# Seven half-size products for eight in the last batch's output stage, and one ring of buffers

## The chip, the cores and the metric

The kernel runs on one core of a Trainium2 chip. The metric is the device time of one execution in microseconds: the median of several runs. A profile is one such execution, taken by the hardware profiler; its times are counted from the first instruction.

Engines: PE multiplies matrices and accumulates in PSUM (PEld is its loading of weights, which overlaps the multiplications); DVE works on vectors; ACT does activations and copies; POOL issues most loads here; SP issues the stores and the transposing transfers.

## The reference, cut to what matters

An attention over channels is followed by a gated feed-forward layer. B = 4, N = 5824, C = 256, F = 1024; the output has B * N = 23296 rows of 256.

```python
qn = q / (np.linalg.norm(q, axis=1, keepdims=True) + 1e-06)
kn = k / (np.linalg.norm(k, axis=1, keepdims=True) + 1e-06)
s = kn.transpose(0, 2, 1) @ qn / tau
a = softmax(s, -1)                 # a [C, C] for each batch
x = (v @ a).reshape(B * N, C)
h = ((x @ w1) * (x @ w2)) @ w3     # [B * N, F]
out = (h @ w_out).astype(np.float32)
```

The kernel folds what has no rows in it. The softmax of a batch goes into w1 and w2 (the tile Wf, two matrices of 256 x 1024), and w3 @ w_out is one matrix W of 1024 x 256 (the tile W_sb). What is left for each row is a = v Wf1, b = v Wf2, ab = a * b, out = ab W.

## The kernel before, in words

**Tiles and chunks.** A batch's rows stand in 45 groups of 128 and a rest of 64. A chunk c takes four groups, 512 rows; a batch has eleven such chunks (c = 0 to 10) and a small one (c = 11: the 45th group and the rest). NCH is 12, FT = 8 is the number of blocks of 128 among the 1024 features.

**A slot.** The main loop runs over batches b, chunks c and blocks j = 0 to 7. I call one turn of it a slot. In a slot `emit_ab(b, c, j)` issues four matmuls of 512 columns: a and b for the 128 features of block j, each as a sum over two halves of C. ACT copies a from PSUM to SBUF as bf16 (`as`, L482). DVE multiplies it with b in PSUM and writes ab in bf16 (`abs`, L497): 128 features by 512 rows. The PSUM tag "ab" has four buffers, so a and b of a slot take the place of those two slots earlier; `as` has four buffers.

**The output stage.** `emit_out(b, c, j, ab)` multiplies ab with W: for each of the four groups of rows, ab's 128 x 128 block is loaded as weights and W's 256 columns of block j are streamed (L521). Over the eight j the sums stand in two PSUM tiles of 128 x 2 x 256. After j = 7, ACT copies one (L542) and DVE the other (L543) into `osb`, and SP stores the chunk (L544), 512 KB.

**The order around it.** The order on each engine is the order in which the Python program issues, and tiles' hazards become semaphore waits. Finished ab tiles wait in the list `pend`; a slot pops one when more than LAG = 2 are in it, so the output matmuls of a block stand two slots behind its multiplication. In batch 0, W isn't ready until late, ab tiles pile up, and then two are popped in a slot. In the last two chunks the lag rises to LAG_END = 5, and five entries are left for the end. Other work (loads, the scores and softmax of the next batch, W's computation) is in `agenda`, a list of due times against `clock`, a running sum of planned PE time; `run_due` issues what is due. Loads on POOL stand behind gates (L464, L468): a copy of one element that waits for the newest ab or for a transposed piece.

**Buffers.** q, k and v come in pieces of 1024 rows (4 KB a partition), with 5, 6 and 3 buffers. ab tiles have 34 buffers of 1 KB (tag "ab_sb"); those of the first two chunks take a q buffer for four of them. The transposed w3 takes four k buffers. A buffer is handed out again when the program has issued the last reader of its tile.

Of the kernel before, what the change touches and what calls it, by code (L numbers as in the profile page):

```python
# [12 lines left out]
F32 = DT.float32  # L13
BF16 = DT.bfloat16

P = 128
PIECE = 8
LAG = 2
LAG_END = 5
IN_BUFS = {"q": 5, "k": 6, "v": 3}  # L20
MM_COL = 1.0 / 2400.0
MM_FIX = 0.0025

# [2 lines left out]
def kernel(  # L26
# [12 lines left out]
    nc = tc.nc  # L39

    B, N, C = q.shape
    T, D = out.shape
# [8 lines left out]
    FT = F // P  # L51
    NT = N // P
# [5 lines left out]
    NCH = NT // 4 + 1  # L58
# [6 lines left out]
    in_pool = ctx.enter_context(tc.tile_pool(name="in_pool", bufs=1))  # L65
    vT_pool = ctx.enter_context(tc.tile_pool(name="vT_pool", bufs=2))
    wf_pool = ctx.enter_context(tc.tile_pool(name="wf_pool", bufs=2))
    work = ctx.enter_context(tc.tile_pool(name="work", bufs=2))
    psum = ctx.enter_context(tc.tile_pool(name="psum", bufs=1, space=bass.MemoryType.PSUM))
# [17 lines left out]
    W_sb = consts.tile([P, FT, D], BF16)  # L87
# [12 lines left out]
    pieces = {}  # L100

    def new_piece(nm, n, pi):
        t = in_pool.tile([P, PIECE, C], BF16, tag=nm, name=f"{nm}_{n}_{pi}", bufs=IN_BUFS[nm])
        pieces[nm, n, pi] = t
        if pi == NP_ - 1:
            if nm != "v":
                nc.vector.memset(t[LEFT:, LAST, :], 0.0)
            nc.gpsimd.dma_start(out=t[:LEFT, LAST, :], in_=qk_main[nm, n][1])
# [6 lines left out]
    def load_piece(nm, n, pi, cuts=()):  # L115

        new_piece(nm, n, pi)
        ends = [0, *cuts, LAST if pi == NP_ - 1 else PIECE]
        for lo, hi in zip(ends, ends[1:]):
            load_part(nm, n, pi, lo, hi)  # L120
# [19 lines left out]
    def transpose_half_on_pe(n, pi, h, on_act):  # L140
        if pi == 0 and h == 0:
            new_vT(n)
        t = pieces["v", n, pi]
        i0 = 4 * h
        pe_transpose(
            vTs[n][0][:, pi * PIECE + i0 : pi * PIECE + i0 + 4, :, :].rearrange("p i c t -> p (i c) t"),
            [t[:, i0 + i, ct * P : (ct + 1) * P] for i in range(4) for ct in range(CT)],
            "out", on_act,
        )
# [279 lines left out]
    clock = [0.0]  # L429
# [11 lines left out]
    def at(t, cost, fn):  # L441
        seq[0] += 1
        agenda.append((t, seq[0], cost, fn))
# [3 lines left out]
    pend = []  # L447

    def chunk_cols(c):
        return 4 * P if c < NCH - 1 else P + LEFT  # L450

    def rhs_of(b, c, ct):
        vT, vTt = vTs[b]
        if c < NCH - 1:
            return vT[:, 4 * c : 4 * c + 4, ct, :]
        return vTt[:, ct, :]

    last_ab = [None]
    held = [None]

    def gate():

# [3 lines left out]
    def hold(src):  # L466

        nc.gpsimd.tensor_copy(gate_t, src)  # L468

    def emit_ab(b, c, j):  # L470
        n = chunk_cols(c)
        tiles = []
        for w in range(2):
            t = psum.tile([P, 512], F32, tag="ab", name=f"{'ab'[w]}_{b}_{c}_{j}", bufs=4)
            for ct in range(CT):
                nc.tensor.matmul(  # L476
                    t[:, :n], lhsT=Wf[b][:, ct, w, j * P : (j + 1) * P], rhs=rhs_of(b, c, ct),
                    start=(ct == 0), stop=(ct == CT - 1),
                )
            tiles.append(t)  # L480
        a_sb = work.tile([P, 512], BF16, tag="a_sb", name=f"as_{b}_{c}_{j}", bufs=4)
        nc.scalar.copy(a_sb[:, :n], tiles[0][:, :n])  # L482
        if c == NCH - 1:
            if b % 2 == 0 and j == 0:
                lefts[b // 2] = work.tile([P, FT, 2, P + LEFT], BF16, tag="left", name=f"left_{b}", bufs=1)
            both = lefts[b // 2][:, j, b % 2, :]
            nc.vector.tensor_mul(both, a_sb[:, :n], tiles[1][:, :n])  # L487
            ab = both[:, :P] if b % 2 == 0 else both[:, LEFT:]
        else:
            if b == 0 and c < 2:  # L490

                if j % 4 == 0:
                    held[0] = in_pool.tile([P, 4, 512], BF16, tag="q", name=f"abq_{c}_{j}", bufs=IN_BUFS["q"])
                ab = held[0][:, j % 4, :]
            else:
                ab = work.tile([P, 512], BF16, tag="ab_sb", name=f"abs_{b}_{c}_{j}", bufs=8 * NDEF + 2)
            nc.vector.tensor_mul(ab, a_sb, tiles[1])  # L497
        pend.append((b, c, j, ab))
        last_ab[0] = ab
        clock[0] += 4 * (n * MM_COL + MM_FIX)  # L500

    def emit_out(b, c, j, ab, only=None):
# [42 lines left out]
            if only is None:  # L545
                del out_tiles[b, c]

    NDEF = 4

    def load_qk(n, pi):  # L550
        load_piece("q", n, pi)
        load_piece("k", n, pi)
# [5 lines left out]
    for nm in "kq":  # L558
        new_piece(nm, 0, 0)
        raw[nm] = work.tile([P, half, C], F32, tag="o_sb", name=f"raw_{nm}", bufs=3)  # L560
        first = nc.sync if nm == "k" else nc.scalar
# [8 lines left out]
    def transpose_w3():  # L570

        for h in range(FT // 2):
            m = in_pool.tile([P, 2, FT, P], BF16, tag="k", name=f"w3T_{h}", bufs=IN_BUFS["k"])
            nc.sync.dma_start_transpose(m, w3_bf[:, 2 * h : 2 * h + 2, :])
            w3T.append(m)

# [67 lines left out]
    w_ready = [False]  # L644
# [21 lines left out]
    def make_agenda(b):  # L666
        agenda.clear()
        clock[0] = 0.0
        n = b + 1
        if b == 0:  # L670
            at(0.5, 0.87, soft0[5])
            for i in range(4):
                at((1.7, 2.6, 3.5, 3.9)[i], 0.43, soft0[7 + i])
            at(0.0, 0.0, load_library)
            at(4.6, 0.5, lambda: transpose_half_on_pe(0, 0, 1, False))
            at(7.0, 0.5, lambda: transpose_half_on_pe(0, 1, 0, True))
            at(8.0, 0.5, lambda: transpose_half_on_pe(0, 1, 1, False))
            at(15.0, 0.0, transpose_w3)
            at(15.0, 0.0, lambda: transpose_piece(0, 2))
            for jt in range(FT):  # L680
                at(27.5 + 1.2 * jt, 0.87, lambda jt=jt: w_unit(jt))
            moves = [("qk", 1, 0, 29.0), ("v", 0, 3, 30.0), ("v", 0, 4, 30.5), ("qk", 1, 1, 44.0), ("qk", 1, 2, 45.0)]
            moves += [("qk", 1, 3, 53.0), ("qk", 1, 4, 55.0), ("v", 0, 5, 61.0), ("qk", 1, 5, 73.0)]
            moves += [("v", 1, 0, 88.0), ("v", 1, 1, 98.0), ("v", 1, 2, 120.0), ("qk", 2, 0, 130.0)]
            t0, t1 = 54.0, 113.0
        else:
            moves = [("v", b, 3, 1.0), ("qk", n, 1, 10.0), ("qk", n, 2, 17.0), ("v", b, 4, 26.0), ("qk", n, 3, 38.0)]
            moves += [("v", b, 5, 46.0), ("qk", n, 4, 58.0), ("qk", n, 5, 66.0)]
            moves += [("v", n, 0, 76.0), ("v", n, 1, 86.0), ("v", n, 2, 96.0), ("qk", n + 1, 0, 108.0)]
            moves = [m for m in moves if m[1] < B]  # L690
            t0, t1 = 16.0, 98.0

        before = (0, 2) if b == 0 else None
        for nm, m, pi, t in moves:
            if before is not None and not (nm == "v" and before == (m, pi - 1) == (0, 3)):
                at(t, 0.0, lambda w=before: hold(vTs[w[0]][1][:1, 0, :1] if w[1] == NP_ - 1 else vTs[w[0]][0][:1, w[1] * PIECE, 0, :1]))
            at(t, 0.0, gate)
            if nm == "qk":
                at(t, 0.0, lambda m=m, pi=pi: load_qk(m, pi))
                before = None  # L700
            else:
                at(t, 0.0, lambda m=m, pi=pi: load_piece("v", m, pi))
                at(t + 4.0, 0.0, lambda m=m, pi=pi: transpose_piece(m, pi))
                before = (m, pi)
        if n == B:
            agenda.sort()
            return
        units = score_units(n)
        for i, (cst, fn) in enumerate(units):
            at(t0 + (t1 - t0) * i / len(units), cst, fn)  # L710
        soft = soft_units(n)
        for cst, t, fn in soft:
            at(t1 + 1.0 + t, cst, fn)
        agenda.sort()

    for b in range(B):
        make_agenda(b)
        for c in range(NCH):
            for j in range(FT):
                run_due()  # L720
                emit_ab(b, c, j)
                npop = 0
                lag = LAG
                if b == B - 1 and c >= NCH - 2:
                    lag = LAG_END if c == NCH - 1 else LAG + (LAG_END - LAG) * (j + 1) // FT
                while w_ready[0] and len(pend) > lag and npop < 2:
                    emit_out(*pend.pop(0))
                    npop += 1
                    run_due()
        run_due(1e9)  # L730

    n = len(pend)
    for i, only in [(i, 1) for i in range(n - 1)] + [(i, 0) for i in range(n - 2)] + [(n - 1, 1), (n - 2, 0), (n - 1, 0)]:
        emit_out(*pend[i], only=only)


# [33 lines left out]
```

## Time and profile before

| what | value |
|---|---|
| time, median of 6 runs | 569.57 us (569.38 to 569.7) |
| the profiled execution | 569.68 us, span 567.9 us |
| PE / PEld busy | 556.7 / 355.4 us |
| DVE / ACT / POOL busy | 375.3 / 339.1 / 78.5 us |
| output matmuls (L521) of 256 columns | 1344 + 64 + 48, mean 273 ns |
| a and b matmuls of 512 columns (L476) | 704 + 704, mean 379 ns |
| ab multiplication (L497) | 687 ns |
| copy of a (L482, 512 columns) | 585 ns |
| granted clock of TensorE | 1.000 |

How to read it: a matmul's duration runs from its start to the end of its last result; matmuls that follow each other start closer than that, and the busy time of a group counts the time that they cover together. In rows of the profile the arrow points from what is read to what is written, the shapes are partitions x elements, and "idle before" names what the engine waited for.

### The profile page before, as it was taken

The numbers are of one execution on the slowest core, as the hardware profiler recorded it, in microseconds if no ns is written. First come the engines' busy times: TensorE is split into PE (matmuls) and PEld (weight loads), VectorE is DVE, ScalarE is ACT, GpSimd is POOL, SyncE is SP. The second block draws the span as 40 slices with busy tenths as digits, with TensorE's granted clock in tenths as the row PEclk, the third lists the DMA queues.
The fourth block names the chain that finished last, engine by engine and source line by source line (L and its number), as shares of the span: only waits on it lengthen the run. The fifth ranks groups of instructions, "written<-read, shape, count | busy, mean of one in ns | idle before, by whom it ended". The sixth has DMA issues, their size and how long they took to land.

```text
span 567.9 us, 10088 instructions
## 1 busy us (share of the span) xinstructions
PE 556.7 (98%) x3748; PEld 355.4 (63%) x3755; DVE 375.3 (66%) x581; ACT 339.1 (60%) x627; POOL 78.5 (14%) x163
## 2 busy tenths in 40 slices
PE   8799999999999999999999999999999999999997
PEld 5664576776656666666656666666665666566655
DVE  1047645888966578888766667787876665565564
ACT  1047536777766577777575567777765554454453
POOL 4260013120211010121210101030120000000000
PEclk9999999999999999999999999999999999999999
DMA  9999989978455696595661495765741325221011
GB/s 213 211 178 208 169 173 233 228 165 196 114 146 121 140 194 147 91 191 124 146 149 75 96 220 117 156 120 122 184 113 39 85 74 149 63 66 72 38 69 61
DMA packets 75105, 77.45 MB, mean 136 GB/s; under 512 B 54193, under 2 KB 58801, under 8 KB 75057
## 3 DMA queue, kind: packets, MB, share of 16 engines
q0 software_dynamic: 15760, 38.93, 39.4%
q1 hardware_dynamic: 59008, 37.23, 21.5%
q10 hardware_dynamic: 288, 0.66, 0.4%
q8 instruction: 29, 0.48, 0.4%
q14 instruction: 20, 0.16, 0.1%
HBM read 78.91 MB, written 23.86 MB: 181 GB/s over the span
## 4 chain that ended last, share of the span: by engine, by line
PE 93%; DMA 5%; ACT 1%; POOL 0%; issue 0%; DVE 0%; ACTq 0%; POOLq 0%
PE o L521 28%; PE a L476 28%; PE b L476 28%; PE G L192 5%; DMA k<-in_k_dram 5%; PE fold L363 2%; PE w L649 1%; ACT kr L283 0%; PE quarter L389 0%; POOL k L111 0%; POOL q L111 0%; PE sqk L225 0%; PE tr_I-594_595 L134 0%; PE row L271 0%; ACT e L322 0%
## 5 line engine op out<-in xcount | busy, mean ns | idle before, releaser
L497 DVE TENSOR_TENSOR abs<-as,b 128x512 bf16<-128x512 bf16 x336 | 230.4, 687 | 144.0 <-ACT as L482 131.5
L482 ACT CAST as<-a 128x512 bf16<-128x512 f32 (+1 forms) x384 | 216.3, 563 | 170.1 <-DVE abs L497 84.6
L476 PEld LDWEIGHTS <-Wf 128*128 128x128 bf16 x1536 | 149.1, 98 | 102.2 <-ACT Wf L398 0.7
L476 PE MATMUL a<-vT,Wf 128*128 128x512 bf16 x704 | 209.4, 379 | 0.5 <-ACT Wf L398 0.4
L476 PE MATMUL b<-vT,Wf 128*128 128x512 bf16 x704 | 209.4, 379 | 0.0
L521 PE MATMUL o<-W_sb,abs 128*128 128x256 bf16 x1344 | 201.5, 273 | 0.0
L521 PEld LDWEIGHTS <-abs 128*128 128x128 bf16 x1344 | 131.4, 98 | 79.7 <-issue 0.2
L201 DVE TENSOR_TENSOR acc<-acc,sq 128x1024 f32<-128x1024 f32 x66 | 80.4, 1219 | 0.6 <-ACT sq L189 0.6
L192 PE MATMUL G<-k,q 128*128 128x256 bf16 x276 | 49.7, 273 | 0.0
L189 ACT ACTIVATE sq<-q 128x512 f32<-128x512 bf16 x66 | 41.8, 633 | 0.0
L189 ACT ACTIVATE sq<-k 128x512 f32<-128x512 bf16 x66 | 41.5, 629 | 0.0
L464 POOL COPY gate_t<-abs 1x1 bf16<-1x1 bf16 x39 | 10.5, 270 | 169.4 <-DVE abs L497 167.0
L543 DVE COPY osb<-o 128x512 f32<-128x512 f32 x44 | 30.1, 685 | 0.9 <-PE o L521 0.9
L192 PEld LDWEIGHTS <-q 128*128 128x128 bf16 x276 | 27.0, 98 | 3.1
L542 ACT COPY osb<-o 128x512 f32<-128x512 f32 x44 | 25.8, 586 | 4.0 <-PE o L521 2.1
L468 POOL COPY gate_t<-vT 1x1 bf16<-1x1 bf16 x16 | 3.3, 208 | 162.2 <-DMA vT<-v 162.2
L111 POOL DMA_DIRECT2D q<-in_q_dram x28 | 15.2, 542 | 12.4 <-DMA k<-in_k_dram 5.4
L370 ACT ACTIVATE Wf<-fold,rs 128x512 bf16<-128x512 f32 x15 | 10.3, 687 | 10.9 <-PE fold L363 7.9
L283 ACT ACTIVATE kr<-row 128x256 f32<-128x256 f32 x1 | 0.4, 384 | 26.1 <-PE row L271 26.1
L487 DVE TENSOR_TENSOR left<-as,b 128x192 bf16<-128x192 bf16 x32 | 11.3, 354 | 5.1 <-ACT as L482 2.7
L363 PE MATMUL fold<-w,e 128*128 128x512 bf16 x52 | 14.2, 379 | 0.0
L497 DVE TENSOR_TENSOR abq<-as,b 128x512 bf16<-128x512 bf16 x16 | 10.8, 686 | 5.0 <-ACT as L482 4.5
(98 smaller groups left out, 241.5 us busy)
## 6 DMA issues: line engine op xcount, KB each, us to landing
out_dram<-osb SPq DMA_DIRECT2D x44, 512.0 KB, 3.3
k<-in_k_dram POOLq DMA_DIRECT2D x19, 512.0 KB, 8.5
v<-in_v_dram POOLq DMA_DIRECT2D x19, 512.0 KB, 5.3
q<-in_q_dram POOLq DMA_DIRECT2D x18, 512.0 KB, 6.0
w_wout<-in_moe_w_dram POOLq DMA_DIRECT2D x1, 2048.0 KB, 23.3
k<-in_k_dram POOLq DMA_DIRECT2D x4, 320.0 KB, 7.9
v<-in_v_dram POOLq DMA_DIRECT2D x4, 320.0 KB, 5.0
q<-in_q_dram POOLq DMA_DIRECT2D x3, 320.0 KB, 4.2
```

The source lines that it names most:

```text
L111: nc.gpsimd.dma_start(out=pieces[nm, n, pi][:, lo:hi, :], in_=qk_main[nm, n][0][:, pi * PIECE + lo : pi * PIECE + hi, :])
L189: nc.scalar.activation(out=dst[:, :, part, :], in_=src[:, o : o + 2, :], func=AF.Square)
L192: nc.tensor.matmul(G[:, ct, :], lhsT=qt[:, i, ct * P : (ct + 1) * P], rhs=kt[:, i, :], start=(pr == 0 and part == 0 and ct == 0), stop=(pr ...
L201: nc.vector.tensor_add(accs[n], accs[n], sqs[0])
L363: nc.tensor.matmul(m, lhsT=st["e"][:, c2, c1 * P : (c1 + 1) * P], rhs=w12[:, c2, w, lo:hi], start=(c2 == 0), stop=(c2 == CT - 1),)
L476: nc.tensor.matmul(t[:, :n], lhsT=Wf[b][:, ct, w, j * P : (j + 1) * P], rhs=rhs_of(b, c, ct), start=(ct == 0), stop=(ct == CT - 1),)
L482: nc.scalar.copy(a_sb[:, :n], tiles[0][:, :n])
L487: nc.vector.tensor_mul(both, a_sb[:, :n], tiles[1][:, :n])
L497: nc.vector.tensor_mul(ab, a_sb, tiles[1])
L521: nc.tensor.matmul(tl[h][:, o, :], lhsT=lhsT, rhs=W_sb[:, j, :], start=(j == 0 and o == 0), stop=(j == FT - 1 and (small or o == 1)), skip ...
L542: nc.scalar.copy(o[:, 0:2, :], tl[0])
L543: nc.vector.tensor_copy(o[:, 2:4, :], tl[1])
```

## The change

In chunks 0 to 9 of the last batch the product ab W is formed by a scheme of seven products of half the size for eight (Winograd's form of Strassen's method). ab W is seen as a 2 x 2 block matrix product: A is 512 rows by 1024 features, halved to A11, A12 (256 rows; features 0 to 511, 512 to 1023), A21, A22 (the other 256 rows), and W is halved to B11, B12, B21, B22 (512 features by 128 columns). Each product is four blocks of features times two groups of rows: eight matmuls of 128 columns, with weights of their own, in place of thirty-two of 256 columns for a chunk in all.

- **Sums of ab**: S1 = A21 + A22, S2 = S1 - A11, S3 = A11 - A21, S4 = A12 - S2, four DVE operations on 128 x 1024 bf16. S1 is issued in slot 7 of the chunk itself, S2, S3 and S4 with the products p1, p5 and p7, which stand two, two and three slots ahead of the reader (p6, p7, p3); p5 reads S1.
- **Sums of W** (`combine_weights`): five DVE subtractions and two ACT copies, in four steps that batch 1's agenda has at 3.0, 5.6, 8.2 and 10.8.
- **Products**: in the order p1, p5, p6, p7, p2, p4, p3, one in each of slots 0 to 6 of the next chunk, after that slot's a and b; slot 7 has none. They accumulate in three PSUM tiles: A gets p1, then p6, p7 and p4 on top of each other, C gets p5 and then p3 on top, B gets p2.
- **Quarters of the output**: `keep` copies A (ACT) into a quarter of `osb` after p1, p6, p7 and p4; `join` adds a PSUM tile to a quarter (DVE): B to (0,0) after p2, C to (1,1) in p4's slot ahead of p4, C to (0,1) after p3. Then the chunk is stored as before.
- **The list**: an entry of `pend` now carries the slot from which it may be popped and a size; a slot has room for two; a product has size 2.
- **Buffers**: q, k and v pieces, the transposed w3, ab (now in halves of four blocks, 4 KB) and the sums share one tag of 22 buffers of 4 KB.

The diff, cut:

```diff
-IN_BUFS = {"q": 5, "k": 6, "v": 3}
+BIG_BUFS = 22
...
-        t = in_pool.tile([P, PIECE, C], BF16, tag=nm, name=f"{nm}_{n}_{pi}", bufs=IN_BUFS[nm])
+        t = in_pool.tile([P, PIECE, C], BF16, tag="big", name=f"{nm}_{n}_{pi}", bufs=BIG_BUFS)
...
+    def seven(b, c):
+        return b == B - 1 and c < NCH - 2
+
+    def combine_weights(step):
...
+        if step == 0:
+            nc.vector.tensor_sub(f[:, 0], b12, b11)
+        elif step == 1:
+            nc.scalar.copy(T[:, 0], f[:, 0])
+            nc.vector.tensor_sub(f[:, 1], b22, f[:, 0])
+        elif step == 2:
+            nc.scalar.copy(T[:, 1], f[:, 1])
+            nc.vector.tensor_sub(T[:, 2], b22, b12)
+        else:
+            nc.vector.tensor_sub(T[:, 3], b21, f[:, 1])
+
+    def seven_products(b, c, k1, k2):
...
+        a11, a21 = k1[:, :, : 2 * P], k1[:, :, 2 * P :]
+        a12, a22 = k2[:, :, : 2 * P], k2[:, :, 2 * P :]
...
+        def product(nm, a, w, first=False):
+            if first:
+                st[nm] = psum.tile([P, 2, P], F32, tag="out", name=f"prod{nm}_{b}_{c}", bufs=3)
+            for j in range(4):
+                for i in range(2):
+                    nc.tensor.matmul(
+                        st[nm][:, i, :], lhsT=a[:, j, i * P : (i + 1) * P], rhs=w[j],
+                        start=(first and j == 0 and i == 0), stop=(j == 3), skip_group_check=True,
+                    )
...
+        def keep(r, d):
+            nc.scalar.copy(quarter(r, d), st["A"])
+
+        def join(nm, r, d):
+            nc.vector.tensor_add(quarter(r, d), st[nm], quarter(r, d))
+
+        def sum1():
+            nc.vector.tensor_add(s1, a21, a22)
+
+        def p1():
+            st["o"] = work.tile([P, 4, D], F32, tag="o_sb", name=f"osb_{b}_{c}", bufs=3)
+            nc.vector.tensor_sub(s2, s1, a11)
+            product("A", a11, w1, True)
+            keep(0, 0)
+
+        def p5():
+            nc.vector.tensor_sub(s3, a11, a21)
+            product("C", s1, t1, True)
+
+        def p6():
+            product("A", s2, t2)
+            keep(0, 1)
+
+        def p7():
+            nc.vector.tensor_sub(s4, a12, s2)
+            product("A", s3, t3)
+            keep(1, 1)
+
+        def p2():
+            product("B", a12, w21, True)
+            join("B", 0, 0)
+
+        def p4():
+            join("C", 1, 1)
+            product("A", a22, t4)
+            keep(1, 0)
+
+        def p3():
+            product("C", s4, w22)
+            join("C", 0, 1)
+            rows = out[b * N : b * N + NT * P, :].rearrange("(p i) c -> p i c", i=NT)
+            nc.sync.dma_start(out=rows[:, 4 * c : 4 * c + 4, :], in_=st["o"])
+
+        return [sum1, p1, p5, p6, p7, p2, p4, p3]
...
-            if b == 0 and c < 2:
-
-                if j % 4 == 0:
-                    held[0] = in_pool.tile([P, 4, 512], BF16, tag="q", name=f"abq_{c}_{j}", bufs=IN_BUFS["q"])
-                ab = held[0][:, j % 4, :]
-            else:
-                ab = work.tile([P, 512], BF16, tag="ab_sb", name=f"abs_{b}_{c}_{j}", bufs=8 * NDEF + 2)
+            if j % 4 == 0:
+                halves[j // 4] = in_pool.tile([P, 4, 512], BF16, tag="big", name=f"abh_{b}_{c}_{j}", bufs=BIG_BUFS)
+            ab = halves[j // 4][:, j % 4, :]
             nc.vector.tensor_mul(ab, a_sb, tiles[1])
-        pend.append((b, c, j, ab))
...
+        slot[0] += 1
+        if not seven(b, c):
+            pend.append((slot[0] + LAG, 1, lambda only=None: emit_out(b, c, j, ab, only)))
+        elif j == FT - 1:
+            fns = seven_products(b, c, *halves)
+            fns[0]()
+            pend.extend((slot[0] + 1, 2, fn) for fn in fns[1:])
...
+        if b == 1:
+            for i in range(4):
+                at(3.0 + 2.6 * i, 0.0, lambda i=i: combine_weights(i))
...
-                lag = LAG
+                lag = 0
...
-                while w_ready[0] and len(pend) > lag and npop < 2:
-                    emit_out(*pend.pop(0))
-                    npop += 1
+                room = 2
+                while w_ready[0] and len(pend) > lag and pend[0][0] <= slot[0] and pend[0][1] <= room:
+                    _, size, fn = pend.pop(0)
+                    fn()
+                    room -= size
                     run_due()
```

More of the change, by code (lines that the diff above doesn't have):

```diff
@@ L458 @@
     last_ab = [None]
-    held = [None]
+    halves = [None, None]
+    slot = [0]
+    comb = {}
+    def seven(b, c):
+        return b == B - 1 and c < NCH - 2
+    def combine_weights(step):
+        b11, b12 = W_sb[:, 0:4, :P], W_sb[:, 0:4, P:]
+        b21, b22 = W_sb[:, 4:8, :P], W_sb[:, 4:8, P:]
+        if step == 0:
+            comb["T"] = in_pool.tile([P, 4, 4, P], BF16, tag="big", name="comb_T", bufs=BIG_BUFS)
+            for nm in ("S12", "S34"):
+                comb[nm] = in_pool.tile([P, 2, 4, 2 * P], BF16, tag="big", name=f"comb_{nm}", bufs=BIG_BUFS)
+            comb["f"] = in_pool.tile([P, 2, 4, P], F32, tag="big", name="comb_f", bufs=BIG_BUFS)
+        T, f = comb["T"], comb["f"]
+        if step == 0:
+            nc.vector.tensor_sub(f[:, 0], b12, b11)
[7 more added lines that the diff above has]
+            nc.vector.tensor_sub(T[:, 3], b21, f[:, 1])
@@ new lines, in seven_products, with quarter @@
+    def seven_products(b, c, k1, k2):
+        T = comb["T"]
+        a11, a21 = k1[:, :, : 2 * P], k1[:, :, 2 * P :]
+        a12, a22 = k2[:, :, : 2 * P], k2[:, :, 2 * P :]
+        s1, s2 = comb["S12"][:, 0], comb["S12"][:, 1]
+        s3, s4 = comb["S34"][:, 0], comb["S34"][:, 1]
+        w1 = [W_sb[:, j, :P] for j in range(4)]
+        w21 = [W_sb[:, 4 + j, :P] for j in range(4)]
+        w22 = [W_sb[:, 4 + j, P:] for j in range(4)]
+        t1, t2, t3, t4 = ([T[:, i, j, :] for j in range(4)] for i in range(4))
+        st = {}
+        def product(nm, a, w, first=False):
[7 more added lines that the diff above has]
+                    )
+            clock[0] += 8 * (P * MM_COL + MM_FIX)
+        def quarter(r, d):
+            return st["o"][:, 2 * r : 2 * r + 2, d * P : (d + 1) * P]
+        def keep(r, d):
[32 more added lines that the diff above has]
+        return [sum1, p1, p5, p6, p7, p2, p4, p3]
@@ L546, in emit_out @@
                 del out_tiles[b, c]
-    NDEF = 4
     def load_qk(n, pi):
@@ L572, in transpose_w3 @@
         for h in range(FT // 2):
-            m = in_pool.tile([P, 2, FT, P], BF16, tag="k", name=f"w3T_{h}", bufs=IN_BUFS["k"])
+            m = in_pool.tile([P, 2, FT, P], BF16, tag="big", name=f"w3T_{h}", bufs=BIG_BUFS)
             nc.sync.dma_start_transpose(m, w3_bf[:, 2 * h : 2 * h + 2, :])
@@ L721 @@
                 emit_ab(b, c, j)
-                npop = 0
-                lag = LAG
+                lag = 0
                 if b == B - 1 and c >= NCH - 2:
                     lag = LAG_END if c == NCH - 1 else LAG + (LAG_END - LAG) * (j + 1) // FT
-                while w_ready[0] and len(pend) > lag and npop < 2:
-                    emit_out(*pend.pop(0))
-                    npop += 1
+                room = 2
[3 more added lines that the diff above has]
+                    room -= size
                     run_due()
@@ L733 @@
     for i, only in [(i, 1) for i in range(n - 1)] + [(i, 0) for i in range(n - 2)] + [(n - 1, 1), (n - 2, 0), (n - 1, 0)]:
-        emit_out(*pend[i], only=only)
+        pend[i][2](only=only)
 _INS = ['q', 'k', 'v', 'tau', 'moe_w1', 'moe_w2', 'moe_w3', 'moe_w_out']
```

## The prediction, made before the changed kernel had run

> **What bounds the kernel now.** I read the page first: the busy shares and the chain of waits.
>
> ```profile
> PE 556.7 (98%) x3748; PEld 355.4 (63%) x3755; DVE 375.3 (66%) x581; ACT 339.1 (60%) x627; POOL 78.5 (14%) x163
> PE 93%; DMA 5%; ACT 1%; POOL 0%; issue 0%; DVE 0%; ACTq 0%; POOLq 0%
> ```
>
> PE is busy for 98% of the span and carries 93% of the chain. Next, the windows, to see whether this holds in the last batch, where the products change, and in the early stretch in which PE makes a and b without output products:
>
> ```profile
> 38.00:60.00 22.00, 21.95 (x124) 10.95 (x124) 16.15 (x25) 15.63 (x26) 0.40 (x1) 1.00 1.06 192
> 465.00:490.00 25.00, 25.00 (x155) 14.96 (x153) 15.19 (x23) 12.89 (x22) 0.89 (x3) 1.00 0.33 85
> 490.00:515.00 25.00, 25.00 (x155) 15.04 (x154) 14.31 (x22) 12.59 (x22) 1.26 (x3) 1.00 0.33 93
> ```
>
> Columns: stretch, length, busy PE, PEld, DVE, ACT, POOL, granted clock, DMA share, GB/s. PE has no hole in the last batch and its clock is full, so a microsecond taken from its stream there is a microsecond of the kernel, until another engine is late. To see how late the others run I took the timeline of one slot (one call of emit_ab and one of emit_out):
>
> ```profile
> 480.28 0.59 PE L476 MATMUL a<-vT,Wf 128*128 128x512 bf16 x2
> 480.71 0.59 PE L476 MATMUL b<-vT,Wf 128*128 128x512 bf16 x2
> 480.91 0.59 ACT L482 CAST as<-a 128x512 bf16<-128x512 f32 x1 [0.71 <-DVE abs L497]
> 481.14 0.60 PE L521 MATMUL o<-W_sb,abs 128*128 128x256 bf16 x4
> 481.53 0.69 DVE L497 TENSOR_TENSOR abs<-as,b 128x512 bf16<-128x512 bf16 x1 [0.61 <-ACT as L482]
> 481.58 0.59 PE L476 MATMUL a<-vT,Wf 128*128 128x512 bf16 x2
> ```
>
> Columns: start, length, what. A slot lasts 481.58 - 480.28 = 1.30 us: 0.86 for a and b (four matmuls started 0.216 apart) and 0.44 for four output matmuls 0.109 apart. On a slot clock that starts with a, as runs 0.63 to 1.22 and the multiplication 1.25 to 1.94, 0.64 into the next slot. DVE is then idle for 0.61 us.
>
> **PE's part.** A chunk loses 8 x 4 = 32 matmuls of 256 columns, 32 x 0.109 = 3.49 us, and gets 7 x 8 = 56 of 128 columns, each with weights of its own. The kernel has that shape at its start, in the squares and the transposes:
>
> ```profile
> 26.65 1.06 PE L225 MATMUL sqk<-k 128*128 128x128 bf16 x16
> 43.63 0.61 PE L134 MATMUL tr_I-594_595<-ident_b,v 128*128 128x128 bf16 x8
> ```
>
> One such matmul takes 0.219 us, so 16 of them start (1.06 - 0.219)/15 = 0.056 us apart and 8 of them (0.61 - 0.219)/7 = 0.056, all with different weights, between 512-column matmuls too (the transposes stand between a's and b's). 56 x 0.056 = 3.12 us. Saved: 0.37 us a chunk, 3.7 us in ten. The lower bound of the spacing is this row; the upper one is a weight load that overlaps nothing, 0.098 us by its row, 5.49 us a chunk and 20 us in all. I take 0.056, because the row has the very shape. Break-even is 3.49/56 = 0.062 us.
>
> The Trainium skill speaks against it: "TensorE: Matmul & The Clock Gate", section "Back-to-back issue gap", gives about 81 ns per matmul for a sustained stream of weight loads and 128-column matmuls. By that a chunk's products would take 4.54 us, 1.05 more than now, and the kernel 580 us. The rows of this trace say 56 ns, though in runs of 16 at most.
>
> **DVE's part.** A chunk loses one 684 ns copy and gets four sums of 1024 bf16 numbers and three joins (256 f32 from PSUM plus SBUF). For a join there is a row of the same form, for a sum there is none; the nearest are these:
>
> ```profile
> L317 DVE TENSOR_TENSOR s<-G,kr 128x256 f32<-128x256 f32 x8 | 3.2, 416 | 0.2 <-ACT kr L283 0.2
> L138 DVE COPY vT<-tr_I-496_497 128x1024 bf16<-128x1024 bf16 x1 | 0.7, 693 | 0.0
> L201 DVE TENSOR_TENSOR acc<-acc,sq 128x1024 f32<-128x1024 f32 x66 | 80.4, 1219 | 0.6 <-ACT sq L189 0.6
> ```
>
> So a sum takes between 0.69 (1024 bf16, but a copy) and 1.22 us (1024, two operands, but f32). I take 0.69: the type is the sum's. "VectorE: DVE Perf Modes", section "The perf-mode tier table", of the Trainium skill lists a two-operand bf16 operation from SBUF at twice the f32 rate (1224 ns for 2048); as an estimate that is 0.69 us here.
>
> Busy DVE per chunk: 8 x 0.687 + 4 x 0.69 + 3 x 0.416 = 9.5 us of about 10.1, after 6.2 of 10.4. That is tight, but independent operations start before the one in front ends (a copy follows a multiplication 0.61 us after its start, at 498.43 and 499.04), which brings the sum to 8.3. The order within the chunk decides, so I walk it. Slots 0 to 6 now last 0.86 + 0.45 = 1.31 us, slot 7, without a product, 0.86: a chunk is 7 x 1.31 + 0.86 = 10.03 us. Clock from the start of slot 7:
> - sum1 needs the multiplication just before it, so it starts 0.03 after 1.94 (dependent DVE pairs here start 34 ns after the first ends): 1.97 to 2.66. p5 reads it at 0.86 + 1.31 + 0.86 = 3.03. Spare 0.37.
> - The next multiplication starts at 2.58, 0.5 late; s2 runs 3.19 to 3.88, p6 reads it at 4.34. Spare 0.46.
> - The next is at 3.80; s3 runs 4.41 to 5.10, p7 reads it at 5.65. Spare 0.55.
> - b's buffers are reused two slots on: a multiplication may end 1.09 late (0.66 across slot 7) before PE waits for it; it is 0.5 late.
>
> The joins: in slot 5 the join of C (quarter 1,1) stands behind that slot's multiplication: it starts at 1.25 + 0.61 = 1.86, ends at 2.27, with some 0.04 to the waiter (the step from a's end to as) 2.31. p3 writes C and would start at 1.31 + 0.86 = 2.17. **PE waits 0.14 us** in every chunk. Behind p3 stand the next slot's a and b, so everything after it moves by that: 1.4 us in ten chunks. Below, it could be nothing, if DVE gets to the join earlier; above, 0.26, if it doesn't overlap the multiplication and starts 0.03 after it. The other two joins wait for products that ended 0.4 us before DVE is free, and their readers are slots away.
>
> **ACT's part.** Four keeps of 372 ns (L538's form) for one copy of 586: 0.9 us more a chunk, 6.2 of 10.1. The tightest is p6's: the product ends at 1.31 + 0.16 = 1.47, keep runs 1.51 to 1.88, p7 writes that PSUM tile at 2.17 (spare 0.29) and as of the next slot is due at 1.94. No cost; a keep of 0.586 us would still fit.
>
> **What else moves.** combine_weights: five subtractions (at most 0.69 each) and two ACT copies (about 0.63) in batch 1, one step in 2.6 us; each takes at most DVE's 0.61 of idle time in its slot, and a multiplication has 1.09 of slack. Nothing; 3.1 us if all fell on PE. The ring: I followed the written order and counted the tiles alive. Of 22 buffers at most 17 are in use in batch 0; later 9, and the four of the combined weights. Buffers are handed out in the order in which they came free, so a new tile waits for readers long done. POOL gets no new instruction, its gates stand as before; SP still issues one output transfer a chunk, after the join in slot 6. Before, piece q(0,5) waited for a buffer and now doesn't, but the loads there wait for landings with the DMA at its limit: nothing. Chunk 0 has six slots of 0.86 without output work; the window 38 to 60 shows PE full in such slots. The list of deferred work is again five entries long when the last product starts, so the tail stays.
>
> **The sum.** The profiled execution took 569.68 us (567.9 of span, 1.8 around it), the median is 569.57, so the sum applies to both. 569.57 - 3.7 + 1.4 = **567.3 us**, 0.4% less. With the wait between nothing and 0.26 a chunk: 565.9 to 568.5.
>
> **Rivals.**
> - *Slow sums* (slower): a sum takes the f32 row's 1.22 us. Then s1 ends at 3.19 and p5 waits 0.20; s2 ends at 4.94 against 4.54, 0.44 with the step to PE; s3 at 6.69 against 6.29, 0.44. With p3's 0.14 a chunk is 11.25 us, 0.85 over now: 578 us. It decides from the point at which s3 is late: s3 ends at 3.03 + 3 x (a sum), which meets p7 at 0.86 us, and the whole gain is gone at 0.94. For it: no row with two bf16 operands. Against it: the 693 ns row.
> - *No wait at p3*: 565.9 us. For it: only an overlap larger than the rows show.
> - *New waits eat the gain*: two more waits of p3's size a chunk, from handovers between engines that the walk leaves 0.3 to 0.5 of spare: 567.3 + 2 x 1.4 = 570.1 us, and 568.7 with one. For it: DVE at 94% by durations.
> - *Paced by weight loads*: from 0.062 us on the products cost more than now; halfway to the 0.098 row, at 0.077, a chunk is 0.82 over now: 578 us. The 56 ns rows speak against it.
>
> **Chances.** Forecast (566.4 to 568.5) 0.60, no wait 0.11, new waits 0.14 (half of it within 0.2%), slow sums 0.10, weight loads 0.05. About 0.2% (1.1 us) is what a measurement of this kernel can tell from no change: faster 0.71, same 0.08, slower 0.21. The range takes the first two whole and the new waits up to 570.2, and leaves out 0.19: 565.6 to 570.2; the likeliest case alone is 566.4 to 568.5.
>
> **What would show it.** In the changed profile: 80 matmuls for each of the seven products at 0.056 us spacing; a sum near 0.69 us; idle PE before p3 of about 0.14 us ten times, released by the join; p5, p6 and p7 without idle time; batches 0 to 2 as long as before. Sums over 0.86 us, or products more than 0.062 us a matmul, would prove the forecast wrong; idle PE at p7 or p2 would show a handover that I took to be covered.

## The result, and the profile after

The changed kernel takes 568.19 us (median of 20 runs) against 569.52 us for the kernel before (40 runs): a ratio of 0.9977, 95% interval 0.9971 to 0.9983. It is faster by 0.23%, or 1.33 us, where the forecast had 2.3. The profiled execution took 567.97 us, its span is 566.2 us.

The changed kernel's busy shares and its chain of waits, from the page:

```profile
PE 554.5 (98%) x3988; PEld 355.3 (63%) x3995; DVE 403.4 (71%) x645; ACT 349.2 (62%) x659; POOL 78.2 (14%) x163
PE 93%; DMA 5%; ACT 1%; POOL 0%; issue 0%; DVE 0%; ACTq 0%; POOLq 0%
```

DVE has 28 us more work than before (375.3) and PE still makes up 93% of the chain. The windows, in two of the stretches that were shown of before (the columns are the same):

```profile
38.00:60.00 22.00, 21.46 (x120) 10.60 (x120) 16.12 (x24) 14.95 (x26) 0.04 (x1) 1.00 1.04 188
465.00:490.00 25.00, 25.00 (x219) 15.38 (x217) 21.70 (x38) 14.97 (x30) 0.89 (x3) 1.00 0.41 85
```

Two things are to be seen. In the last batch DVE is now busy for 21.70 of 25 us (15.19 before), and PE still looks full. In the first row, which is in batch 0 and far from any product, PE has lost half a microsecond: 21.46 against 21.95.

**Where the time went.** I took the start of each slot's first matmul in both traces and compared the distances between them. That shows waits that busy times hide.

| stretch | before | after | difference |
|---|---|---|---|
| batch 0, start of chunk 1 to start of chunk 3 | 13.93 | 14.74 | +0.81 |
| batch 3, start of chunk 0 to start of chunk 1 | 9.74 | 7.12 | -2.62 |
| batch 3, each of the next nine chunks | 10.40 | 10.18 | -0.22 |
| batch 3, start of chunk 10 to start of chunk 11 | 9.09 | 11.06 | +1.97 |
| batch 3, from there to the last a | 5.11 | 5.54 | +0.43 |

The second row is six slots without output matmuls, 6 x 0.44 us; the last two rows give nearly all of it back, because the same work stands later. Over all of the last batch the difference is -2.62 - 9 x 0.22 + 1.97 + 0.43 = -2.2 us. With the +0.81 of batch 0 and +0.06 between batch 0's chunk 3 and the start of the last batch that is -1.3 us: the measured difference of the medians. The two spans differ by 0.38 more, because the first a starts at 37.49 in the trace of before and at 37.11 here; in the traces of the experiments below it starts between 37.13 and 37.70, so a difference of that size at the start comes without any of these edits; I take it for chance.

The chunk's length, 10.18 us, is the predicted 10.03 + 0.14. So the last batch did what the sum said, and the error sits in batch 0. There the ring of buffers had been costed at nothing. The timeline at that place (start, length, what, and the idle time before it), first of the kernel before, where the a of slot 3 of chunk 2 follows b after 0.43 us, and then of the changed kernel:

```profile
57.61 0.59 PE L476 MATMUL b<-vT,Wf 128*128 128x512 bf16 x2
58.04 0.59 PE L476 MATMUL a<-vT,Wf 128*128 128x512 bf16 x2
```

```profile
57.24 0.59 PE L574 MATMUL b<-vT,Wf 128*128 128x512 bf16 x2
...
57.44 0.59 ACT L580 CAST as<-a 128x512 bf16<-128x512 f32 x1 [0.28 <-PE a L574]
...
58.08 0.59 PE L574 MATMUL a<-vT,Wf 128*128 128x512 bf16 x2 [0.24 <-ACT as L580]
...
58.71 0.59 ACT L580 CAST as<-a 128x512 bf16<-128x512 f32 x1 [0.68 <-PE a L574]
...
59.34 0.59 PE L574 MATMUL a<-vT,Wf 128*128 128x512 bf16 x2 [0.24 <-ACT as L580]
```

The first a was due at 57.24 + 0.43 = 57.67 and starts at 58.08, 0.05 after the ACT copy of the slot directly before it has ended. So this a waits for the buffer of the slot before, not of the one two slots before. The same happens at 59.34. Each time PE loses 0.41 us.

The trace also records for which engine's semaphore each instruction waits, and this bears the reading out. In chunk 2 of before, every a waits for ACT's semaphore and every b for DVE's: a takes a buffer that a copy has read, b one that a multiplication has read. In the changed kernel the b of slots 2, 5 and 6 wait for ACT's and the a of slots 5, 6 and 7 for DVE's: b has taken a buffer that an a had, and the other way round. So the statement that a and b take the place of those two slots earlier doesn't hold in this chunk. Such exchanges stand in a few other slots too, also in the kernel before, where the list of waits shows no loss; what costs is that an a gets a buffer that was read only just before.

### The profile page after: what moved, and what is told of

Same layout as the page of the kernel before. It is cut to its first block, busy times and chain, and to the rows that moved or that the text cites. A ratio compares the mean times of both kernels' runs of the same rounds, so it can differ in the third digit from the quotient of the medians.

```text
span 566.2 us, 10693 instructions
## 1 busy us (share of the span) xinstructions
PE 554.5 (98%) x3988; PEld 355.3 (63%) x3995; DVE 403.4 (71%) x645; ACT 349.2 (62%) x659; POOL 78.2 (14%) x163
## 4 chain that ended last, share of the span: by engine, by line
PE 93%; DMA 5%; ACT 1%; POOL 0%; issue 0%; DVE 0%; ACTq 0%; POOLq 0%
PE a L574 28%; PE b L574 28%; PE o L621 22%; PE G L192 5%; DMA k<-in_k_dram 5%; PE prodA L505 3%; PE fold L363 2%; PE prodC L505 2%; PE w L747 1%; PE prodB L505 1%; ACT kr L283 0%; PE quarter L389 0%; POOL k L111 0%; ACT as L580 0%; POOL q L111 0%
## 5 line engine op out<-in xcount | busy, mean ns | idle before, releaser
L591 DVE TENSOR_TENSOR abh<-as,b 128x512 bf16<-128x512 bf16 x352 | 240.8, 686 | 118.0 <-ACT as L580 111.6
L574 PEld LDWEIGHTS <-Wf 128*128 128x128 bf16 x1536 | 146.1, 98 | 104.0 <-issue 1.7
L621 PE MATMUL o<-W_sb,abh 128*128 128x256 bf16 x1088 | 161.4, 273 | 0.0
L621 PEld LDWEIGHTS <-abh 128*128 128x128 bf16 x1088 | 106.3, 98 | 61.1 <-issue 0.2
L562 POOL COPY gate_t<-abh 1x1 bf16<-1x1 bf16 x39 | 10.6, 271 | 170.6 <-DVE abh L591 168.3
L505 PEld LDWEIGHTS <-comb_S 128*128 128x128 bf16 x320 | 21.2, 98 | 11.0 <-issue 2.7
L643 DVE COPY osb<-o 128x512 f32<-128x512 f32 x34 | 23.3, 685 | 0.9 <-PE o L621 0.9
L515 ACT COPY osb<-prodA 128x256 f32<-128x256 f32 x40 | 14.9, 373 | 11.7 <-PE prodA L505 11.7
L642 ACT COPY osb<-o 128x512 f32<-128x512 f32 x34 | 19.9, 586 | 3.4 <-PE o L621 1.6
L505 PEld LDWEIGHTS <-abh 128*128 128x128 bf16 x240 | 15.9, 98 | 7.1
```

The costliest lines, as they stand in the source:

```text
L505: nc.tensor.matmul(st[nm][:, i, :], lhsT=a[:, j, i * P : (i + 1) * P], rhs=w[j], start=(first and j == 0 and i == 0), stop=(j == 3), skip_ ...
L515: nc.scalar.copy(quarter(r, d), st["A"])
L574: nc.tensor.matmul(t[:, :n], lhsT=Wf[b][:, ct, w, j * P : (j + 1) * P], rhs=rhs_of(b, c, ct), start=(ct == 0), stop=(ct == CT - 1),)
L621: nc.tensor.matmul(tl[h][:, o, :], lhsT=lhsT, rhs=W_sb[:, j, :], start=(j == 0 and o == 0), stop=(j == FT - 1 and (small or o == 1)), skip ...
L642: nc.scalar.copy(o[:, 0:2, :], tl[0])
L643: nc.vector.tensor_copy(o[:, 2:4, :], tl[1])
```

## The experiments

My theory after the two traces: the ring costs 0.81 us by these two waits and nothing else, the seven products bring 2.2 us, and about 1.4 us more is lost to the wait for `join("C", 1, 1)` ahead of p3.

**The ring alone.** The kernel before, with nothing of the change but the shared buffers (for k, the transposed w3 and ab as for q):

```diff
-IN_BUFS = {"q": 5, "k": 6, "v": 3}
+BIG_BUFS = 22
...
-            if b == 0 and c < 2:
...
-            else:
-                ab = work.tile([P, 512], BF16, tag="ab_sb", name=f"abs_{b}_{c}_{j}", bufs=8 * NDEF + 2)
+            if j % 4 == 0:
+                halves[j // 4] = in_pool.tile([P, 4, 512], BF16, tag="big", name=f"abh_{b}_{c}_{j}", bufs=BIG_BUFS)
+            ab = halves[j // 4][:, j % 4, :]
```

> The kernel before with the one ring of 22 buffers and nothing else of the change. Theory (the ring has a price in batch 0: in the third chunk the PSUM buffers of a and b are handed out in another order, and PE waits twice for the copy of a of the slot just before, 0.40 us each, as in the changed kernel's trace at 58.08 and 59.34): 0.8 us slower than before, 570.3 us, with both waits in the trace and a and b of every later slot 0.8 us later. Rival (the ring costs nothing, as predicted, and the missing 0.9 us is lost in the last batch): 569.5 us, no shift.

Measured: 570.43 us against 569.60, ratio 1.0013 (1.0004 to 1.0022), so 0.83 us slower (0.2 to 1.3 by the interval). Its timeline has the same two waits, the same a and b wait for the other engine's semaphore, and the way from chunk 1 to chunk 3 takes 14.75 us:

```profile
58.30 0.59 PE L476 MATMUL a<-vT,Wf 128*128 128x512 bf16 x2 [0.24 <-ACT as L482]
...
59.57 0.59 PE L476 MATMUL a<-vT,Wf 128*128 128x512 bf16 x2 [0.24 <-ACT as L482]
```

The loss needs nothing of the products: the ring by itself brings it.

**Two buffers of their own for the ab halves of chunk 2.** The changed kernel, in which the two halves that batch 0's chunk 2 writes don't come from the ring:

```diff
-BIG_BUFS = 22
+BIG_BUFS = 20
...
-                halves[j // 4] = in_pool.tile([P, 4, 512], BF16, tag="big", name=f"abh_{b}_{c}_{j}", bufs=BIG_BUFS)
+                tag, bufs = ("own", 2) if b == 0 and c == 2 else ("big", BIG_BUFS)
+                halves[j // 4] = in_pool.tile([P, 4, 512], BF16, tag=tag, name=f"abh_{b}_{c}_{j}", bufs=bufs)
```

> The changed kernel with two buffers of their own for the two ab halves of batch 0's third chunk (20 in the ring). Theory (the ring's price): both waits go and the time falls by 0.8 us to 567.4 us, 2.1 below before, which is the predicted saving of the last batch alone. Rival (the loss is in the last batch): 568.2, as the changed kernel.

Measured: 567.38 us, ratio 0.9956 (0.9944 to 0.9968), 0.81 us under the changed kernel. From chunk 1 to chunk 3 it takes 13.95 us, and its timeline at that place has no wait left:

```profile
57.45 0.59 PE L574 MATMUL b<-vT,Wf 128*128 128x512 bf16 x2
57.88 0.59 PE L574 MATMUL a<-vT,Wf 128*128 128x512 bf16 x2
...
58.74 0.59 PE L574 MATMUL a<-vT,Wf 128*128 128x512 bf16 x2
```

So where the ab half lies decides in which order the PSUM buffers of a and b are handed out. In the changed kernel those two a's take the buffers of the slot before; here they don't: every a of chunk 2 waits for ACT's semaphore again, and every b for DVE's. Nor do the waits look like a shortage of buffers in SBUF: there are 22 in all here too, and what the two a's waited for were copies out of PSUM. The first multiplication into a half that lay in a piece's buffer carries one more wait, on a load that landed long before. The order that came of it is the one that would fit if that first multiplication ended only after the copies of slots 0 to 2, which it doesn't in the trace. Whether the program reckoned with such a late end is not tested; how the extra wait leads to another order stays open.

**The join a slot earlier.** The changed kernel with one line moved from p4 to p2, one slot earlier and ahead of p2's own join:

```diff
         def p2():
+            join("C", 1, 1)
             product("B", a12, w21, True)
             join("B", 0, 0)
 
         def p4():
-            join("C", 1, 1)
             product("A", a22, t4)
```

> The changed kernel with the join of quarter (1,1) issued a slot earlier, ahead of p2 in place of ahead of p4. DVE's work and PE's stay the same. Theory (p3 waits 0.145 us because this join stands behind its slot's multiplication): a chunk falls from 10.18 to 10.03 us, ten chunks by 1.4 us, 566.8 us. Rival (DVE's total of 9.5 us a chunk sets the pace, not one join's place): the wait moves to another matmul and the time stays at 568.2.

Measured: 566.66 us, ratio 0.9940 (0.9928 to 0.9953), 1.53 us under the changed kernel; a chunk takes 10.03 us, and the way from chunk 1 to chunk 3 still 14.74.

**Both together.** The last two edits in one kernel:

> Both edits, two buffers of their own and the early join. If the two losses are separate they add: 568.2 - 0.8 - 1.4 = 566.0 us, 3.5 below before, near the 3.7 us that the matmuls alone save. If they share a cause, no more than the larger: 566.8.

Measured: 565.88 us, ratio 0.9926 (0.9914 to 0.9939). The two parts add up: 0.81 + 1.53 = 2.34 us expected, 568.19 - 565.88 = 2.31 measured. A chunk takes 10.03 us, the way from chunk 1 to chunk 3 13.94 us. PE's timeline at p3, and below it DVE's, in this kernel:

```profile
459.97 0.59 PE L574 MATMUL b<-vT,Wf 128*128 128x512 bf16 x2
460.40 0.61 PE L505 MATMUL prodC<-W_sb,comb_S 128*128 128x128 bf16 x8
```

```profile
458.77 0.42 DVE L518 TENSOR_TENSOR osb<-prodC,osb 128x256 f32<-128x256 f32 x1
```

The join of C has ended at 459.19, 1.2 us before p3 starts; p3 follows b after 0.43 us, without a wait. This kernel takes 0.74% less than the kernel before, with each part of the change in it; none here has a lower median, and only the last one below has the same.

**Each sum issued twice.** The changed kernel with a second copy of each of the four sums:

```diff
         def sum1():
             nc.vector.tensor_add(s1, a21, a22)
+            nc.vector.tensor_add(s1, a21, a22)
...
             nc.vector.tensor_sub(s2, s1, a11)
+            nc.vector.tensor_sub(s2, s1, a11)
...
             nc.vector.tensor_sub(s3, a11, a21)
+            nc.vector.tensor_sub(s3, a11, a21)
...
             nc.vector.tensor_sub(s4, a12, s2)
+            nc.vector.tensor_sub(s4, a12, s2)
```

> The changed kernel with each of the four sums issued twice in a row, which makes a sum 0.61 + 0.69 = 1.30 us long. Theory (the order within the chunk decides, the walk of the prediction): s1 ends at 3.27 and p5 waits 0.28; s2 ends at 5.10 and p6 waits 0.52; s3 at 6.93 and p7 waits 0.52; p3 at least 0.14: a chunk takes 11.5 to 11.7 us in place of 10.18, ten chunks 13 to 15 us more, 581 to 583 us. Rival (only DVE's total counts, from start to start 8.3 + 4 x 0.61 = 10.7 us a chunk): 0.55 us a chunk, 574 us.

Measured: 587.43 us against 569.57, ratio 1.0312 (1.0296 to 1.0328); a chunk takes 12.12 us. That is beyond both expectations, but on the side of the walk through the chunk. DVE's timeline shows why the size was off:

```profile
501.77 0.69 DVE L521 TENSOR_TENSOR comb_S<-abh,abh 128x1024 bf16<-128x1024 bf16 x1
502.49 0.69 DVE L522 TENSOR_TENSOR comb_S<-abh,abh 128x1024 bf16<-128x1024 bf16 x1
503.10 0.68 DVE L595 TENSOR_TENSOR abh<-as,b 128x512 bf16<-128x512 bf16 x1
```

The second copy writes the same tile and waits for DVE's own semaphore; it starts 0.72 us after the first, that is 0.03 after the first has ended; the independent multiplication behind it starts 0.61 after it. So a pair lasts 0.72 + 0.69 = 1.41 us, not the 1.30 of two operations that overlap. PE's timeline in the same chunk:

```profile
502.40 0.59 PE L578 MATMUL b<-vT,Wf 128*128 128x512 bf16 x2
503.24 0.62 PE L505 MATMUL prodC<-comb_T,comb_S 128*128 128x128 bf16 x8 [0.24 <-DVE comb_S L522]
...
505.17 0.62 PE L505 MATMUL prodA<-comb_T,comb_S 128*128 128x128 bf16 x8 [0.44 <-DVE comb_S L527]
...
507.10 0.62 PE L505 MATMUL prodA<-comb_T,comb_S 128*128 128x128 bf16 x8 [0.44 <-DVE comb_S L533]
...
511.47 0.61 PE L505 MATMUL prodC<-W_sb,comb_S 128*128 128x128 bf16 x8 [0.27 <-DVE osb L518]
```

p5 was due 0.43 after b, at 502.83, and starts at 503.24: it waits 0.41 us. In the same way p6 waits 0.61 and p7 0.61; p3 waits 0.44, since DVE has no idle time between the doubled s4 and the join. Together that is 2.07 us a chunk, 1.92 more than in the changed kernel; a chunk is 1.94 longer. Each wait starts where the walk has it: at p5, p6, p7 and p3, released by the sum or the join that the walk names. The order within the chunk decides, not DVE's total: DVE still has 7% of idle time (23.35 us busy of 25.00), and with 0.72 in place of 0.61 for the second copy the rival's total would be 8.3 + 4 x 0.72 = 11.2 us, under the 12.12 measured.

**Rings apart.** The kernel with the early join, in which q, k, v, w3 and the sums keep a ring of 13, and the ab halves get one of 9:

```diff
-BIG_BUFS = 22
+BIG_BUFS = 13
...
-                halves[j // 4] = in_pool.tile([P, 4, 512], BF16, tag="big", name=f"abh_{b}_{c}_{j}", bufs=BIG_BUFS)
+                halves[j // 4] = in_pool.tile([P, 4, 512], BF16, tag="abr", name=f"abh_{b}_{c}_{j}", bufs=9)
```

> The changed kernel with the early join and with the ring parted: nine buffers for the ab halves, thirteen for the pieces, the transposed w3 and the sums; the same 22 in all. Theory (only the handout in batch 0 costs, and it comes from ab halves that take buffers over from pieces): as with both edits, 565.9 us. Rival (fewer buffers for the pieces hold up loads, which one ring avoids): PE waits for pieces, over 567 us.

Measured: 565.88 us, ratio 0.9934 (0.9922 to 0.9947), no different from the kernel with both edits. The way from chunk 1 to chunk 3 takes 13.94 us, so the two waits are gone here too, and in chunk 2 a and b wait for the same semaphores as before. The profiled execution is the slowest of this kernel's five (566.54; the others 565.6 to 565.9). Its timeline has one wait for a load, in chunk 0, which takes 0.86 us longer than elsewhere:

```profile
45.48 0.62 PE L134 MATMUL tr_I-615_616<-ident_b,v 128*128 128x128 bf16 x8 [0.69 <-DMA v<-in_v_dram]
```

The other four times, 0.6 to 0.9 us shorter, hardly have room for it, so the smaller ring doesn't seem to hold the loads up as a rule; their traces aren't known.

## Why the prediction was right in its sign and 0.9 us off in its size

That 568.19 us lies within the stated range is in part luck: the upper part of the range stood for a longer wait at p3 and for new waits in the last batch, and the 0.8 us came from a term that had been put at nothing.

**Products: right.** Eight matmuls of 128 columns cover 0.61 us, so they start (0.61 - 0.219)/7 = 0.056 us apart, as taken. With all waits at p3 gone a chunk takes 10.03 us against 10.40 before: 0.37 us saved, the predicted size. (56 x 0.056 is 3.14 us, not the 3.12 of the prediction; from start to start the trace gives the 0.37.) The spacing of 81 ns, which the Trainium skill ("TensorE: Matmul & The Clock Gate", section "Back-to-back issue gap") gives for a sustained stream, would have meant 1.05 us a chunk more; here 560 matmuls with weights of their own kept to 56 ns, in runs of eight between wider ones. The rival *paced by weight loads* falls.

**Sums: right.** The groups of DVE in the last batch (count, busy time, mean ns, idle time before):

```profile
L521 DVE TENSOR_TENSOR comb_S<-abh,abh 128x1024 bf16<-128x1024 bf16 x10 | 6.9, 692 | 0.3
L538 DVE TENSOR_TENSOR comb_S<-abh,comb_S 128x1024 bf16<-128x1024 bf16 x10 | 6.8, 685 | 0.0
L525 DVE TENSOR_TENSOR comb_S<-comb_S,abh 128x1024 bf16<-128x1024 bf16 x10 | 6.8, 684 | 0.0
L530 DVE TENSOR_TENSOR comb_S<-abh 128x1024 bf16<-128x1024 bf16 x10 | 6.8, 683 | 0.0
```

0.683 to 0.692 us, where 0.69 was taken from a copy's row. *Slow sums* falls. The estimate from the Trainium skill ("VectorE: DVE Perf Modes", section "The perf-mode tier table") was 0.69 us too, and these rows agree with it.

**The wait at p3: right, and hidden from two views.** PE's timeline of the changed kernel, and then DVE's:

```profile
460.02 0.59 PE L574 MATMUL a<-vT,Wf 128*128 128x512 bf16 x2
460.45 0.59 PE L574 MATMUL b<-vT,Wf 128*128 128x512 bf16 x2
461.04 0.61 PE L505 MATMUL prodC<-W_sb,comb_S 128*128 128x128 bf16 x8
```

```profile
459.96 0.69 DVE L591 TENSOR_TENSOR abh<-as,b 128x512 bf16<-128x512 bf16 x1 [0.29 <-ACT as L580]
460.57 0.42 DVE L518 TENSOR_TENSOR osb<-prodC,osb 128x256 f32<-128x256 f32 x1
```

p3 was due at 460.45 + 0.43 = 460.88 and starts at 461.04, 0.05 after the join has ended (460.57 + 0.42 = 460.99). The join stands behind the multiplication and starts 0.61 after it, as the walk had it. 0.15 us against the predicted 0.14, and the early join turned ten of them into 1.53 us. Yet PE's line shows no idle time, and the list of waits has no entry for p3: b's last results come out until 461.04, so PE counts as busy up to the very start of p3. The prediction had asked for "idle PE before p3"; that sign doesn't show. Only start-to-start distances show it, or the chain of the changed kernel, where p3 has the length of a product and the wait together:

```profile
459.74 0.45 PE prodA L505 x8
...
461.05 0.60 PE prodC L505 x8
```

**p5, p6, p7: right.** None of them waits in the changed kernel: all steps from b to product but p3's are 0.43 to 0.44 us. The doubled sums put their waits at the predicted readers.

**The ring: this step failed.** It was costed at "Nothing", since "a new tile waits for readers long done". That is true of the SBUF buffers, and no PE wait for a load or a piece came with it. The step looked no further than the buffers that were being merged. The walk took it as given that "b's buffers are reused two slots on"; that was read off the last batch, where it held. In batch 0's chunk 2 the ring changes the order in which the four PSUM buffers of a and b go round, and two a's had to wait for the ACT copy one slot before: 2 x 0.41 = 0.81 us against nothing, shown with the ring alone (+0.83 us) and with two halves taken out of it (-0.81 us). The sum with that term is 567.3 + 0.8 = 568.1 us; 568.19 was measured. The semaphores of chunk 2 differ from those of before in just the kernels that have this loss. Why the program hands the buffers out in this order stays open. The rival *new waits* named the right kind of loss, a handover between engines, but in the wrong place: not in the chunks of the last batch, but once, in a batch that the products don't touch. "Batches 0 to 2 as long as before" was the sign that failed.

**Start-up, W's sums and the tail: right, as far as the traces go.** From batch 0's chunk 3 to the start of the last batch the traces of before and after differ by 0.06 us, and the list of deferred work still ends with the same twelve matmuls. W's sums are four subtractions, not the five of the change's description and the prediction; in the trace they take 0.42 to 0.68 us each, in batch 1, and the two copies 0.62.

## What to carry to other kernels

A change of buffers is not costed by the buffers alone: where a framework hands out all tiles from the program's order, a merge in SBUF can reorder another memory's buffers, as it did here, and what has to be compared is which earlier reader each tile waits for, in every stage. When PE seems full, measure start-to-start distances of the same slot in both traces: a wait shorter than the time by which a matmul's results trail its successor's start (0.16 us here) shows in no busy time and in no list of waits. And with many short dependent steps, walk the order within one period: moving one addition by a slot was worth 1.53 us, more than the whole change had brought.

## What the runs showed of the hardware that I had not expected

- The list of waits understates each wait on PE by the tail of the matmul ahead: the two waits in batch 0 are listed at 0.24 us and cost 0.41; those of p6 and p7 with doubled sums at 0.44 and cost 0.61; the one at p3, of 0.15, is not listed.
- On DVE a second write to the same tile, which the program makes wait for DVE's own semaphore, starts 0.72 us after the first, against 0.61 for an independent operation of the same length. Whether the engine would overlap the two without that wait no run here shows.
